# A decode attention kernel: SyncE's wait for the output moved behind the block, and W_O loaded in five pieces

## The chip, the cores and the metric

The kernel runs on one core of one Trainium2 chip, as one launch. The metric is the device time of that launch in microseconds (us); of several runs the median is taken. A profiled execution is one more run, with a trace; its span reaches from the first to the last instruction of the program.

The core has five engines that work beside each other: TensorE (PE in the profile, its weight loads PEld), VectorE (DVE), ScalarE (ACT), GpSimd (POOL) and SyncE (SP). [...] Transfers between the chip's memory and the on-chip buffers are issued by SyncE or ScalarE, run on 16 DMA engines, and add 16 to a semaphore when all of their data have landed.

## The reference

One token for each of four sequences (B = 4, D = 512) passes a layer norm and then an attention branch and a gated feed-forward branch in parallel; the output is the sum of the input and of both branches. Attention has 32 query heads on 8 key/value heads of 128, over the last 4096 positions of a cache of 16384.

```python
x  = A_x
xn = layernorm(x)
q  = (xn @ wq)  -> [4, 32 heads, 1, 128]
k, v = the last W = 4096 positions of k_cache, v_cache, each kv head used by 4 query heads
p  = softmax(q @ k^T * 128**-0.5)
attention   = (p @ v) -> [4, 1, 4096] @ wo        # wo: 4096 x 512
feedforward = (silu(xn @ w_gate) * (xn @ w_up)) @ w_down   # F = 1792
out = x + attention + feedforward                 # [4, 1, 512], bf16
```

## The kernel before

The keys and values of two sequences and one kv head make one step; there are ND = 16 steps. A step's keys are 2 MB and its values 2 MB, each loaded with one transfer into one half of a double buffer (`kbuf`, `vbuf`). TensorE turns the keys (`transposes`), VectorE copies them out of PSUM, TensorE forms the scores against the queries, VectorE finds the row maximum, ScalarE takes the exponential, and TensorE multiplies with the values (`pv`). TensorE and VectorE run this in a loop of eight rounds of two steps, one step behind each other in a software pipeline.

All weights and all keys and values are issued by SyncE, in the order in which its function in the block is written: W_Q, two steps of keys, the two feed-forward weights W_gate and W_up, then values and keys in turn, each behind the wait that frees its half buffer, then W_down, the last step's values in two halves, and W_O. No scheduler moves anything: every engine's order is the order of its function.

W_O is held as 32 rows of 512 elements in each of 128 partitions (4 MB; a row is 1 KB in a partition and 128 KB in all). `WO_CUTS` (L120) says where it is cut. Before, the cuts (0, 16, 26, 30, 32) make four pieces of 16, 10, 4 and 2 rows. Each piece is one transfer (`load_wo`, L227 to L229) with a semaphore of its own, `d_wo[n]`. At the end of TensorE's function (L479 to L486) a loop over the 32 rows waits for a piece where a cut stands, and adds two matmuls for each row (the two halves of the 512 output columns) into `ps_acc`, which already holds the input and the feed-forward branch. Behind the first piece four unneeded matmuls (`spin`) fill a pause.

When the last matmul is done (`s_acc`), VectorE casts `ps_acc` into `y` (L349), and SyncE (L247) and ScalarE (L267) issue one output transfer each, of 2 KB. Both add 16 to `d_out`, and SyncE waits for 32 (L248) as the last step of its function. The wait on L248 is carried by the branch with which SyncE leaves the block; the profile shows it with line 171.

Behind the five functions the block (`with nc.Block()`, L171) ends with a barrier: each of the other engines drains and adds to a semaphore, GpSimd collects these, and then releases all. In the profile all of this has line 171. The program's first barrier, ahead of the block, has line 500.

Of the kernel before, what the change touches and what calls it, by code (L numbers as in the profile page):

```python
# [10 lines left out]
def bass_parallel_sum__sliding_block_cached__swiglu_ffn__decode_kernel(  # L11
# [10 lines left out]
    out: bass.AP,  # L22
):
    B, _, D = A_x.shape
    _, HKV, Sk, Dh = A_k_cache.shape
    HQ = A_wq.shape[1] // Dh
    F = B_w_gate.shape[1]
# [84 lines left out]
    def sem(name):  # L112
        return nc.alloc_semaphore(name=name)
# [3 lines left out]
    d_wu = sem("d_wu")  # L117
    d_wd = sem("d_wd")
    d_out = sem("d_out")
    WO_CUTS = (0, 16, 26, 30, 32)  # L120
    d_wo = [sem("d_wo%d" % q) for q in range(len(WO_CUTS) - 1)]
    d_k = [sem("d_k%d" % s) for s in range(2)]
    d_v = [sem("d_v%d" % s) for s in range(2)]
# [43 lines left out]
    def kv_ap(cache, d):  # L167
        b0 = d % 2 * 2
        return cache[b0:b0 + 2, d // 2, Sk - W:, :].rearrange("b (q t) d -> q b (t d)", t=NT)

    with nc.Block() as block:  # L171
# [40 lines left out]
        @block.sync  # L212
        def _(eng):
            def load_k(d):
                if d >= 2:
                    eng.wait_ge(s_tr, 2 * NG * (d - 1))
                eng.dma_start(KB[:, d % 2 * KVN:(d % 2 + 1) * KVN], kv_ap(A_k_cache, d)).then_inc(d_k[d % 2], 16)

            def load_v(d):
                eng.wait_ge(s_pv, d + 1)  # L220
                eng.dma_start(VB[:, d % 2 * KVN:(d % 2 + 1) * KVN], kv_ap(A_v_cache, d)).then_inc(d_v[d % 2], 16)

            def load_v_half(d, h, done):
                a = d % 2 * KVN + h * HKN
                eng.dma_start(VB[:, a:a + HKN], kv_ap(A_v_cache, d)[:, :, h * HKN:(h + 1) * HKN]).then_inc(done, 16)  # L225

            def load_wo(n):  # L227
                a, b = WO_CUTS[n], WO_CUTS[n + 1]
                eng.dma_start(WO[:, a:b, :], wo_ap[:, a:b, :]).then_inc(d_wo[n], 16)  # L229

            eng.dma_start(WQ[:], wq_ap).then_inc(d_wq, 16)
            load_k(0)
            load_k(1)
            eng.dma_start(WG[:], wg_ap).then_inc(d_wg, 16)
            eng.dma_start(WU[:], wu_ap).then_inc(d_wu, 16)
            load_v(0)
            for d in range(2, ND):
                load_k(d)
                load_v(d - 1)
            eng.dma_start(WD[:], wd_ap).then_inc(d_wd, 16)  # L240
            eng.wait_ge(s_pv, ND)
            load_v_half(ND - 1, 0, d_v[1])
            load_v_half(ND - 1, 1, d_vz)
            for n in range(len(d_wo)):
                load_wo(n)
            eng.wait_ge(s_y, 1)
            eng.dma_start(out_ap[0], y[0:B, :]).then_inc(d_out, 16)  # L247
            eng.wait_ge(d_out, 32)  # L248

        @block.scalar  # L250
        def _(eng):
# [100 lines left out]
        def _(eng):  # L352
# [67 lines left out]
            def spin(n):  # L420

                for _ in range(n):
                    mm(ps_S[0][:], ident[:], KB[:, 0:512], start=True)
# [55 lines left out]
            for c in range(NO):  # L479
                if c == WO_CUTS[1]:  # L480
                    spin(4)
                if c in WO_CUTS:
                    eng.wait_ge(d_wo[WO_CUTS.index(c)], 16)
                for n in range(2):
                    last = mm(ps_acc[64 * n:64 * n + B, 0:256], OP[:, c, :], WO[:, c, 256 * n:256 * n + 256])
            last.then_inc(s_acc, 1)  # L486


# [1 line left out]
_INS = ['A_x', 'A_k_cache', 'A_v_cache', 'A_wq', 'A_wo', 'B_x', 'B_w_gate', 'B_w_up', 'B_w_down']  # L490
_OUTS = [((4, 1, 512), 'bfloat16')]
# [23 lines left out]
```

## Time and profile before

| what | value |
|---|---|
| time, median of 3 runs | 197.37 us (197.1 to 197.96) |
| the profiled execution's own time | 196.87 us |
| its span, first to last instruction | 195.1 us |
| mean granted TensorE clock | 0.991 |
| bytes read from memory | 81.01 MB, 415 GB/s over the span |
| busy share of the span: PE, PEld, DVE, ACT, POOL | 83%, 72%, 59%, 9%, 5% |

The page has the busy shares, the span in 40 slices, and the chain of work that ended last. Its time starts at the span's start. In the tables of instructions a line such as L354 is that of a helper (`mm`), so groups are told apart by what they write and read: `ps_acc<-wo_sb,oP` are the matmuls with W_O. "SPq" and "ACTq" are the sequencers of SyncE and ScalarE, where issues of transfers, drains, branches and semaphore instructions stand. A number in square brackets behind an instruction is the idle time of its engine before it, and what ended that.

### The profile page before, as it was taken

The numbers are of one execution on the slowest core, as the hardware profiler recorded it, in microseconds if no ns is written. First come the engines' busy times: TensorE is split into PE (matmuls) and PEld (weight loads), VectorE is DVE, ScalarE is ACT, GpSimd is POOL, SyncE is SP. The second block draws the span as 40 slices with busy tenths as digits, with TensorE's granted clock in tenths as the row PEclk, the third lists the DMA queues.
The fourth block names the chain that finished last, engine by engine and source line by source line (L and its number), as shares of the span: only waits on it lengthen the run. The fifth ranks groups of instructions, "written<-read, shape, count | busy, mean of one in ns | idle before, by whom it ended". The sixth has DMA issues, their size and how long they took to land.

```text
span 195.1 us, 7758 instructions
## 1 busy us (share of the span) xinstructions
PE 162.7 (83%) x3466; PEld 140.2 (72%) x3467; DVE 114.9 (59%) x250; ACT 16.6 (9%) x26; POOL 10.3 (5%) x23
## 2 busy tenths in 40 slices
PE   0127999379898989898989898989898989898995
PEld 0113898368887888788878787878787878786752
DVE  1005777237676767676767676767676767675610
ACT  5600101001010101010101010101010101010000
POOL 8930000000000000000000000000000000000000
PEclk9999999789999999999999999999999999999999
DMA  6999999999999999999999999999999999999991
GB/s 222 430 430 430 432 420 437 421 430 430 430 433 430 433 433 430 433 430 433 433 437 430 430 430 430 430 430 430 430 430 430 430 433 433 430 428 420 438 407 68
DMA packets 5934, 81.10 MB, mean 416 GB/s; under 512 B 668, under 2 KB 680, under 8 KB 936
## 3 DMA queue, kind: packets, MB, share of 16 engines
q1 hardware_dynamic: 5912, 81.01, 97.4%
q8 instruction: 5, 0.08, 0.1%
q10 hardware_dynamic: 16, 0.01, 0.0%
q14 instruction: 1, 0.01, 0.0%
HBM read 81.01 MB, written 0.00 MB: 415 GB/s over the span
## 4 chain that ended last, share of the span: by engine, by line
DMA 63%; PE 32%; issue 1%; DVE 1%; SPq 1%; DVEq 0%
DMA kbuf<-in_A_k_cache_dram 48%; PE ps_kt L382 16%; DMA wo_sb<-in_A_wo_dram 9%; PE ps_s L354 8%; DMA wq_sb<-in_A_wq_dram 6%; PE ps_o L354 5%; PE ps_acc L354 2%; PE ps_kt L354 2%; DVE kT L294 1%; SPq L225 1%; DVE kT L282 0%; SPq L229 0%; DVE y_sb L349 0%; DVE qz L285 0%; DVEq L293 0%
## 5 line engine op out<-in xcount | busy, mean ns | idle before, releaser
L294 DVE COPY kT<-ps_kt 128x1024 bf16<-128x1024 bf16 x128 | 79.5, 683 | 25.3 <-PE ps_kt L382 25.3
L382 PE MATMUL ps_kt<-ident,kbuf 128*128 128x128 bf16 x1024 | 62.8, 219 | 10.6 <-DMA kbuf<-in_A_k_cache_dram 10.6
L382 PEld LDWEIGHTS ps_kt<-ident,kbuf 128*128 128x128 bf16 x1024 | 57.3, 98 | 15.8 <-issue 15.7
L354 PE MATMUL ps_o<-p,vbuf 128*128 128x64 bf16 x1120 | 39.2, 195 | 0.0
L354 PEld LDWEIGHTS ps_o<-p,vbuf 128*128 128x128 bf16 x1120 | 36.0, 99 | 1.1
L354 PEld LDWEIGHTS ps_s<-qz,kT 128*128 128x128 bf16 x1024 | 31.7, 98 | 6.7 <-issue 3.6
L354 PE MATMUL ps_s<-qz,kT 128*128 x1024 | 34.9, 192 | 1.3
L299 DVE TENSOR_REDUCE rm<-ps_s 128x8 bf16<-128x512 f32 x17 | 11.8, 692 | 23.7 <-PE ps_s L354 23.7
L263 ACT ACTIVATE p<-ps_s 128x512 bf16<-128x512 f32 x17 | 10.1, 597 | 162.1 <-PE ps_s L354 162.1
L354 PE MATMUL ps_o<-p,ones 128*128 128x128 bf16 (+1 forms) x69 | 7.1, 225 | 4.6 <-DMA vbuf<-in_A_v_cache_dram 3.2
L354 PEld LDWEIGHTS ps_o<-p,ones 128*128 128x128 bf16 x69 | 4.6, 100 | 5.6 <-DMA vbuf<-in_A_v_cache_dram 3.4
L354 PE MATMUL ps_kt<-wq_sb,xnT 128*32 128x512 bf16 x32 | 3.4, 610 | 5.2 <-DMA wq_sb<-in_A_wq_dram 5.2
L359 PE MATMUL ps_acc<-i,xn 4*128 4x4 f32 x4 | 0.6, 254 | 7.4 <-ACT xn L260 7.4
L354 PE MATMUL ps_s<-mkc,mkr 2*128 2x512 bf16 x17 | 6.5, 385 | 0.0
L354 PE MATMUL ps_s<-dg,ones 8*128 8x512 bf16 x17 | 6.5, 385 | 0.0
L354 PEld LDWEIGHTS ps_kt<-wq_sb,xnT 128*32 128x32 bf16 x32 | 1.3, 140 | 6.8 <-issue 6.8
L282 DVE STREAM_TRANSPOSE kT<-ps_kt 128x512 f32<-128x512 f32 x2 | 1.4, 718 | 7.8 <-PE ps_kt L354 7.8
L359 PEld LDWEIGHTS ps_acc<-i,xn 4*128 4x128 f32 x4 | 0.6, 207 | 7.3 <-issue 7.3
L310 DVE TENSOR_REDUCE den<-ps_o 128x8 f32<-128x128 f32 x18 | 4.9, 274 | 1.0 <-PE ps_o L354 1.0
L207 POOL MEMSET vbuf<- 128x6144 f32 x1 | 5.2, 5222 | 0.0
L304 DVE TENSOR_REDUCE m<-ps_acc 8x1 f32<-8x128 f32 x17 | 4.6, 269 | 0.3 <-PE ps_acc L354 0.3
L314 DVE TENSOR_TENSOR oT<-ps_o,den 128x8 f32 (+1 forms) x18 | 3.0, 167 | 2.9 <-issue 2.7
(67 smaller groups left out, 50.0 us busy)
## 6 DMA issues: line engine op xcount, KB each, us to landing
kbuf<-in_A_k_cache_dram SPq DMA_DIRECT2D x16, 2048.0 KB, 12.6
vbuf<-in_A_v_cache_dram SPq DMA_DIRECT2D x15, 2048.0 KB, 11.3
wq_sb<-in_A_wq_dram SPq DMA_DIRECT2D x1, 4096.0 KB, 12.3
vbuf<-in_A_v_cache_dram SPq DMA_DIRECT2D x2, 1024.0 KB, 9.2
wo_sb<-in_A_wo_dram SPq DMA_DIRECT2D x1, 2048.0 KB, 14.4
wg_sb<-in_B_w_gate_dram SPq DMA_DIRECT2D x1, 1792.0 KB, 25.7
wu_sb<-in_B_w_up_dram SPq DMA_DIRECT2D x1, 1792.0 KB, 29.3
wd_sb<-in_B_w_down_dram SPq DMA_DIRECT2D x1, 1792.0 KB, 15.0
```

Of the source, the lines that this page charges most:

```text
L207: eng.memset(VB[:, HKN:].bitcast(FP32), 0.0)
L225: eng.dma_start(VB[:, a:a + HKN], kv_ap(A_v_cache, d)[:, :, h * HKN:(h + 1) * HKN]).then_inc(done, 16)
L263: eng.activation(P[:, d % 2 * PS:d % 2 * PS + SN], ps_S[d % 2][:], ACT.Exp, scale=SCALE).then_inc(s_p, 1)
L282: eng.transpose(qT[:, 512 * n:512 * n + 512], ps_kt[n][:])
L294: eng.tensor_copy(KT[:, u * HKN + 1024 * g:u * HKN + 1024 * (g + 1)], kt_ps[g].rearrange("p a b -> p (a b)")).then_inc(s_ev, 1)
L299: eng.tensor_reduce(RM[:], ps_S[bank][:].rearrange("p (t c) -> p c t", c=C), AX.X, ALU.max).then_inc(s_rm, 1)
L304: eng.tensor_reduce(m8[:], mt_ps, AX.X, ALU.max)
L310: eng.tensor_reduce(den[:], den_ps.rearrange("p (t c) -> p c t", c=C), AX.X, ALU.add)
L314: eng.tensor_tensor(OT[:, 2 * b:2 * b + 2, ds(r * REP, REP)], O_ps.rearrange("p (j h) -> p j h", j=2), den[:].rearrange("p (j h) -> p j h" ...
L354: return eng.matmul(o, l, r, start=start, stop=stop, skip_group_check=True)
L359: last = eng.transpose(xT_ps[:, c * B:(c + 1) * B], xn[:].rearrange("b (p c) -> b c p", c=NC)[:, c, :], I4[:])
L382: last = eng.transpose(kt_ps[g][:, k, :], KB[:, a:a + 128], ident[:])
```

## The change

Two edits. `WO_CUTS` gets five pieces, of 16, 10, 3, 2 and 1 rows, so there is one more transfer, one more semaphore and one more wait in TensorE's loop. And SyncE's wait for `d_out` leaves SyncE's function in the block and stands behind the block, so SyncE passes the block's closing barrier first and waits for the output afterwards.

```diff
@@ -117,7 +117,7 @@
     d_wu = sem("d_wu")
     d_wd = sem("d_wd")
     d_out = sem("d_out")
-    WO_CUTS = (0, 16, 26, 30, 32)
+    WO_CUTS = (0, 16, 26, 29, 31, 32)
     d_wo = [sem("d_wo%d" % q) for q in range(len(WO_CUTS) - 1)]
     d_k = [sem("d_k%d" % s) for s in range(2)]
     d_v = [sem("d_v%d" % s) for s in range(2)]
@@ -245,7 +245,6 @@
                 load_wo(n)
             eng.wait_ge(s_y, 1)
             eng.dma_start(out_ap[0], y[0:B, :]).then_inc(d_out, 16)
-            eng.wait_ge(d_out, 32)
 
         @block.scalar
         def _(eng):
@@ -486,6 +485,9 @@
             last.then_inc(s_acc, 1)
 
 
+    nc.sync.wait_ge(d_out, 32)
+
+
 # ---- launch: one core; inputs and outputs as the reference has them ----
```

## The prediction

> **What bounds the kernel now.** I read the page of the profile first: its span, the row of DMA shares and the chain of work that ended last.
>
> ```profile
> span 195.1 us, 7758 instructions
> DMA  6999999999999999999999999999999999999991
> GB/s 222 430 430 430 432 420 437 421 430 430 430 433 430 433 433 430 433 430 433 433 437 430 430 430 430 430 430 430 430 430 430 430 433 433 430 428 420 438 407 68
> DMA 63%; PE 32%; issue 1%; DVE 1%; SPq 1%; DVEq 0%
> ```
>
> The DMA engines are at 90% or more in 38 of the 40 slices, and the chain is made of transfers for 63%. The kernel streams its data; nothing in the diff changes how many bytes are moved. So only two places can move the time: the last transfers, and what follows them. The chain of work cut to the last stretch shows both ends of that.
>
> ```profile
> 173.79 16.83 DMA wo_sb<-in_A_wo_dram
> 190.62 0.04 issue
> 190.66 2.23 PE ps_acc L354 x32
> 192.89 0.02 issue
> 192.92 0.43 DVE y_sb L349
> ```
>
> The timeline of the same stretch (start, duration, engine, line, operation, count) gives the pieces of W_O one by one. The idle time in brackets stands before the first matmul of a piece and is ended by the landing of that piece.
>
> ```profile
> 187.65 1.91 PE L354 MATMUL ps_acc<-wo_sb,oP 128*4 128x256 bf16 x32
> 190.66 0.96 PEld L354 LDWEIGHTS ps_acc<-wo_sb,oP 128*4 128x4 bf16 x20 [0.62 <-DMA wo_sb<-in_A_wo_dram]
> 190.66 2.21 PE L354 MATMUL ps_acc<-wo_sb,oP 128*4 128x256 bf16 x32
> 191.89 0.31 PEld L354 LDWEIGHTS ps_acc<-wo_sb,oP 128*4 128x4 bf16 x8 [0.27 <-DMA wo_sb<-in_A_wo_dram]
> 192.49 0.09 PEld L354 LDWEIGHTS ps_acc<-wo_sb,oP 128*4 128x4 bf16 x4 [0.29 <-DMA wo_sb<-in_A_wo_dram]
> 192.92 0.43 DVE L349 CAST y_sb<-ps_acc 128x256 bf16<-128x256 f32 x1 [5.54 <-PE ps_acc L354]
> 193.37 0.35 SPq L247 DMA_DIRECT2D out_dram<-y_sb  x1
> 193.38 0.28 ACTq L267 DMA_DIRECT2D out_dram<-y_sb  x1
> ```
>
> TensorE waits for each of the pieces of 10, 4 and 2 rows. The end is therefore: last piece lands (192.49), four matmuls, the cast to y, two output transfers issued at 193.37, their landing, and the barrier that closes the block. That barrier is line 171; its instructions (ns as min/median/max, then first and last start) are the last ones of the trace:
>
> ```profile
> L171 POOLq EVENT_SEMAPHORE  x2: 17/17/17, 195.0 to 195.0; - x2
> L171 ACTq DRAIN  x1: 241/241/241, 193.7 to 193.7; - x1
> L171 SPq COMPARE_BRANCH  x1: 33/33/33, 194.8 to 194.8; - x1
> L171 SPq DRAIN  x1: 13/13/13, 194.9 to 194.9; - x1
> L171 SPq EVENT_SEMAPHORE  x1: 17/17/17, 195.1 to 195.1; - x1
> L171 PEldq EVENT_SEMAPHORE  x1: 51/51/51, 195.1 to 195.1; - x1
> ```
>
> SyncE's branch out of the block carries the wait for d_out and starts at 194.8, when the output has landed. Only then come its drain (194.9), GpSimd's collecting and releasing (195.0) and the five engines' leave (195.1). SyncE's own waits, from the table of waits, say the same in sums:
>
> ```profile
> SPq L247 <- DVE y_sb L349: 18.2, 1, 18.2
> SPq L171 <- DMA out_dram<-y_sb: 1.0, 1, 1.0
> SPq L500 <- PEq L500: 0.7, 1, 0.7
> SPq L171 <- PEq L171: 0.2, 1, 0.2
> ```
>
> **Part one: the wait behind the block.** In the instruction order of the changed program SyncE's branch has no wait, and the wait for d_out is the last instruction in its list, behind the barrier. Nothing is queued behind it on SyncE inside the program, and no other engine waits for it there. What moves: SyncE issues the output at 193.37 for 0.35 us, branches at about 193.72 and reaches its drain at about 193.76. ScalarE's drain, which comes straight behind an issue of the same kind, started at 193.7, took 241 ns and so ended at 193.94, 0.8 us before the output had landed: a drain does not wait for a transfer. I give SyncE's drain the same 241 ns in place of the 13 ns it took when the transfer was over: 194.0. From SyncE's drain to the release the barrier takes 0.2 us, so everyone leaves at 194.2. The output lands at 194.8 as before (0.6 us of cover; were the landing 0.6 us quicker, the barrier would be late instead and the saving would shrink to nothing). SyncE then passes one wait instruction, priced like its other one at 17 ns. The span ended at 195.1, the last instruction being TensorE's of 51 ns; 194.8 to that end is 0.35 us, less 0.02 for the wait instruction: **0.33 us saved in the span**.
>
> There is a second part, outside every view. The profiled execution's own time is 196.87 us with a span of 195.1, so 1.77 us lie before the first and behind the last instruction. Now all five engines come to what follows the program at the same moment, 195.1. After the change four come at 194.2 and SyncE alone at about 194.8. Whatever those four do by themselves before they meet SyncE again then lies beside its wait. No view shows this. Its lower bound is 0 (SyncE has the longest way by itself, or they do not meet). The nearest row for the upper bound is the program's first barrier, line 500: SyncE, the first there, waited 0.7 us for the others to get through it. I take the middle, **0.35 us**, since no row is nearer to one end, and keep 0 and 0.7 for the range. [...]
>
> **Part two: the pieces of 3, 2 and 1 rows.** The sizes and the time to landing of the pieces as they are:
>
> ```profile
> wo_sb<-in_A_wo_dram SPq DMA_DIRECT2D x1, 512.0 KB, 17.6
> wo_sb<-in_A_wo_dram SPq DMA_DIRECT2D x1, 256.0 KB, 17.7
> L229 SPq DMA_DIRECT2D wo_sb<-in_A_wo_dram x4: 432/432/601, 173.1 to 174.7; - x4
> L354 PE MATMUL ps_acc<-wo_sb,oP x64: 269/272/273, 187.7 to 192.6; 128*4 128x256 bf16 x64
> 189.00:190.00 1.00, 1.00 (x15) 0.50 (x10) 0.00 (x0) 0.00 (x0) 0.00 (x0) 1.00 0.97 399
> ```
>
> One more issue on SyncE costs 0.43 us at about 175.1. It is hidden: SyncE then waits 18.2 us for y, and the pieces land 17 us after their issue, so their transfers are far behind the issue. No queue of ScalarE or GpSimd changes.
>
> On TensorE the last piece now brings two matmuls in place of four. A row of W_O is a pair of matmuls; 16 rows took 1.91 us of which the last pair is 0.27, so a row adds (1.91 - 0.27) / 15 = 0.11 us. **0.11 us saved** if the last piece lands when it did. The row before it must then be done: the piece of two rows lands about 0.3 us (one row of transfer, below) earlier and needs 0.22 us of steps, so it is out of the way, with 0.08 to spare. The added wait, for d_wo[4], sits in front of those last two matmuls and holds nothing else back.
>
> Against that stands what a fifth piece costs the transfers. From the starts above, the piece of 4 rows came 1.23 us after the one before it, that of 2 rows 0.60 us after that. By size alone a row is (1.23 - 0.60) / 2 = 0.315 us, which leaves 0.60 - 0.63 = -0.03 us as the fixed cost of a piece: none. The change also makes runs shorter (3 KB, 2 KB and 1 KB in place of 4 KB and 2 KB), and no run of 1 KB of a weight is in this trace. The window from 189 to 190 us (last row: length, busy time of PE, PEld, DVE, ACT and POOL, clock, DMA share, GB/s), in which the shorter runs begin, still moved 399 GB/s at 97% busy, that is 411 at full share; the page gives 430 for most slices, so shorter runs lose at most some 5 to 7%. On the last 6 rows (1.9 us) that is 0 to 0.13 us; I take the middle, **0.06 us lost**. Net for the pieces: 0.05 us saved, between 0.14 saved and 0.02 lost.
>
> **The sum.** 0.33 + 0.35 + 0.05 = 0.73 us off 196.87: 196.14 us for that execution. It lies 0.50 us below the median of the runs (197.37), so I set the sum against the median: 197.37 - 0.73 = **196.64 us**, or 0.37% less. A measurement of this kernel can tell about 0.5%, 0.99 us, from no change: the forecast is "within 0.5%".
>
> **Rivals.** *Only the span gains.* What follows the program is not shortened, because SyncE's own way to the meeting point is the longest. For it: SyncE is the only engine that comes late. Against it: at line 500 SyncE was the early one. 0.33 + 0.05 = 0.38 us: 196.99 us. Also here belongs a change that does not do what it says: a SyncE drain that waits for its own transfer, against which ScalarE's 241 ns stand; that would leave 0.05 us, 197.32.
>
> *The whole of the other engines' spread is hidden.* The four take 0.7 us behind the program as at line 500, and SyncE little: 0.33 + 0.70 + 0.05 = 1.08 us, 196.29 us. For it: every instruction with which SyncE leaves a barrier is short (17 ns, TensorE's 51). Against it: the 0.7 us contain GpSimd's constants, which the end does not have. With 0.14 for the pieces it would be 1.17 us.
>
> *A fixed cost for each piece, on the path.* This one ends slower. If the last pieces were paid one after another, each with the latency of a transfer, the last landing would come later by what the output transfer shows from issue to landing, 194.8 - 193.37 = 1.43 us, less the 0.11 of matmuls; with the gain in the span alone the sum is 1.43 - 0.11 - 0.33 = 0.99 us slower, 198.36 us. It decides from 0.44 us of extra landing time with the span's gain, and from 0.79 with the tail's too. The pieces of 4 and 2 rows speak against it: they came 1.23 and 0.60 us apart, in proportion to size. [...]
>
> **How the numbers follow.** Forecast 0.44; only the span, or less, 0.12; the whole spread hidden 0.36; fixed cost 0.08. The first two are within 0.5%, 0.56 together; the third is faster by more than that, 0.36; the fourth stands at the 0.99 us of the bound and goes to slower, 0.08. The range reaches over the first three cases with the runs' own spread of a few tenths (197.1 to 197.96 around 197.37): 196.0 to 197.4 us; the fixed cost and part of the tails stay outside.
>
> **What would show it.** Right: SyncE's drain of line 171 near 193.7 to 194.0, the releases of the other engines near 194.2, and SyncE's wait for the output as the last instruction, with a span near 194.7 and the time outside the span down from 1.77 to about 1.4 us; five issues of W_O; the last LDWEIGHTS group x2 with the wait before it ending within 0.1 us of 192.49. Wrong: a last piece at 192.9 or later (fixed cost), a SyncE drain that ends with the landing (no saving from the wait), a time outside the span that stays at 1.77 (only the span) or falls below 1.2 (more than I took).

## The result, and the profile after

The changed kernel took 196.33 us (median of 8 runs, 195.88 to 196.62), the kernel before beside it 197.45 us (median of 8 runs, 197.01 to 198.07). The ratio is 0.9947, with a 95% interval of 0.9932 to 0.9962: 1.05 us faster, between 0.75 and 1.34 (the two medians lie 1.12 us apart). That is 0.53%, just over the 0.5% that the prediction had named as the bound; its 196.64 us lies 0.31 us above the measured median.

The profiled execution of the changed kernel took 196.38 us, with this span and these shares in the chain of work that ended last:

```profile
span 195.1 us, 7759 instructions
DMA  6999999999999999999999999999999999999992
DMA 61%; PE 34%; issue 1%; DVE 1%; SPq 1%; DVEq 0%
```

The span is the same 195.1 us as before, though the time is shorter. Two things cancel in it, and the timeline of the end shows the first (start, duration, engine, line, operation, count, idle time before it):

```profile
188.18 1.91 PE L353 MATMUL ps_acc<-wo_sb,oP 128*4 128x256 bf16 x32 [0.54 <-DMA wo_sb<-in_A_wo_dram]
191.14 1.29 PEld L353 LDWEIGHTS ps_acc<-wo_sb,oP 128*4 128x4 bf16 x26 [0.57 <-DMA wo_sb<-in_A_wo_dram]
192.65 0.09 PEld L353 LDWEIGHTS ps_acc<-wo_sb,oP 128*4 128x4 bf16 x4 [0.22 <-DMA wo_sb<-in_A_wo_dram]
192.97 0.08 PEld L353 LDWEIGHTS ps_acc<-wo_sb,oP 128*4 128x4 bf16 x2 [0.23 <-DMA wo_sb<-in_A_wo_dram]
193.28 0.42 DVE L348 CAST y_sb<-ps_acc 128x256 bf16<-128x256 f32 x1 [5.92 <-PE ps_acc L353]
193.74 0.35 SPq L247 DMA_DIRECT2D out_dram<-y_sb  x1
193.74 0.28 ACTq L266 DMA_DIRECT2D out_dram<-y_sb  x1
```

In this execution already the first piece of W_O, which the change leaves alone, came late: TensorE waited 0.54 us for it and started at 188.18, against 187.65 before. The second piece came at 191.14 against 190.66, and the output was issued at 193.74 against 193.37. Behind the issue the order is new. The instructions of the block's closing barrier, and the one behind it (ns as min/median/max, first and last start):

```profile
L171 POOLq EVENT_SEMAPHORE  x2: 17/17/17, 194.3 to 194.4; - x2
L171 ACTq DRAIN  x1: 241/241/241, 194.1 to 194.1; - x1
L171 SPq DRAIN  x1: 168/168/168, 194.1 to 194.1; - x1
L171 SPq EVENT_SEMAPHORE  x1: 17/17/17, 194.5 to 194.5; - x1
L171 PEldq EVENT_SEMAPHORE  x1: 51/51/51, 194.5 to 194.5; - x1
```

```profile
L488 SPq EVENT_SEMAPHORE  x1: 17/17/17, 195.1 to 195.1; - x1
```

SyncE drains at 194.1, all engines leave the barrier at 194.5, and the last instruction of the span is SyncE's wait at 195.1. From the issue of the output to the end of the span it was 195.1 - 193.37 = 1.73 us before and is 195.1 - 193.74 = 1.36 us now: 0.37 us less. SyncE's waits show the cover that was left:

```profile
SPq L247 <- DVE y_sb L348: 18.1, 1, 18.1
SPq L488 <- DMA out_dram<-y_sb: 0.6, 1, 0.6
SPq L171 <- PEq L171: 0.2, 1, 0.2
```

When SyncE had passed the barrier it still waited 0.6 us for the output, where it had waited 1.0 us ahead of the barrier. And the time outside the span, 196.87 - 195.1 = 1.77 us before, is 196.38 - 195.1 = 1.28 us.

### The profile page after: what moved, and what is told of

Same layout as the page of the kernel before. It is cut to its first block, busy times and chain, and to the rows that moved or that the text cites. A ratio compares the mean times of both kernels' runs of the same rounds, so it can differ in the third digit from the quotient of the medians.

```text
span 195.1 us, 7759 instructions
## 1 busy us (share of the span) xinstructions
PE 164.4 (84%) x3466; PEld 141.5 (73%) x3467; DVE 115.4 (59%) x250; ACT 16.6 (9%) x26; POOL 10.3 (5%) x23
## 4 chain that ended last, share of the span: by engine, by line
DMA 61%; PE 34%; issue 1%; DVE 1%; SPq 1%; DVEq 0%
DMA kbuf<-in_A_k_cache_dram 46%; PE ps_kt L381 17%; DMA wo_sb<-in_A_wo_dram 9%; PE ps_s L353 8%; DMA wq_sb<-in_A_wq_dram 6%; PE ps_o L353 5%; PE ps_kt L353 2%; PE ps_acc L353 2%; DVE kT L293 1%; SPq L225 1%; DVE kT L281 0%; SPq L229 0%; DVE y_sb L348 0%; DVE qz L284 0%; DVEq L292 0%
## 5 line engine op out<-in xcount | busy, mean ns | idle before, releaser
L381 PE MATMUL ps_kt<-ident,kbuf 128*128 128x128 bf16 x1024 | 65.4, 224 | 10.5 <-DMA kbuf<-in_A_k_cache_dram 10.4
L381 PEld LDWEIGHTS ps_kt<-ident,kbuf 128*128 128x128 bf16 x1024 | 59.9, 100 | 15.8 <-issue 15.7
L353 PE MATMUL ps_o<-p,vbuf 128*128 128x64 bf16 x1120 | 38.4, 193 | 0.0
L353 PEld LDWEIGHTS ps_o<-p,vbuf 128*128 128x128 bf16 x1120 | 35.2, 98 | 1.1
```

The lines of the kernel that those rows point to most:

```text
L353: return eng.matmul(o, l, r, start=start, stop=stop, skip_group_check=True)
L381: last = eng.transpose(kt_ps[g][:, k, :], KB[:, a:a + 128], ident[:])
```

## The experiments

The first theory was the prediction's, with its open term read from the trace after: the wait saves 0.37 us in the span and 0.5 us outside it, the pieces almost nothing. The rivals: the pieces carry most of the gain, or any waiting engine would do as well as SyncE, or each piece has a fixed cost. The ratios are to the kernel before on the same chip, with 95% intervals; "outside" is the mean over the runs of time less span, which is 1.73 and 1.74 us for the kernel before in the two sets.

| run | ratio to before | median us | before us | outside us |
|---|---|---|---|---|
| wait only | 0.9965 (0.9947 to 0.9982) | 196.27 | 197.11 | 1.24 |
| wait only, again | 0.9968 (0.9950 to 0.9986) | 196.42 | 197.20 | 1.25 |
| pieces only | 0.9982 (0.9967 to 0.9997) | 196.94 | 197.11 | 1.75 |
| the change again | 0.9956 (0.9932 to 0.9981) | 196.30 | 197.20 | 1.27 |
| TensorE waits | 0.9973 (0.9957 to 0.9989) | 196.60 | 197.11 | 1.56 |
| rows 16 to 31 singly | 0.9979 (0.9967 to 0.9991) | 196.81 | 197.11 | 1.27 |
| pieces 16, 10, 5, 1 | 0.9972 (0.9955 to 0.9989) | 196.70 | 197.20 | 1.27 |

**The wait alone.** The changed kernel with the old cuts.

```diff
-    WO_CUTS = (0, 16, 26, 29, 31, 32)
+    WO_CUTS = (0, 16, 26, 30, 32)
```

> The wait behind the block, W_O in the old four pieces. Theory 1 (the wait saves about 0.37 us in the span and about 0.5 us outside it, the pieces next to nothing): ratio 0.9957, between 0.994 and 0.997, time outside the span 1.3 us. Rival (the wait saves only the barrier in the span, and the five pieces the rest of the 1.12 us): ratio 0.998, outside the span 1.7 us or more.

The ratio is 0.9965, the medians lie 0.84 us apart, and the time outside the span falls to 1.24 us as in the full change. From the issue of the output to the end of the span its profile has 194.9 - 193.52 = 1.38 us, again some 0.35 us less than before. The rival, in which the tail stays at 1.7 us, is out. The same kernel was run again in the second set:

> The wait behind the block with the old four pieces, once more. Theory 1: 0.85 us faster than before, ratio 0.9957 (0.9945 to 0.997), 1.27 us outside the span. Rival (the pieces carry 0.35 us, so the wait 0.7): ratio 0.9965.

It came out at 0.9968 and 0.78 us between the medians, with 1.25 us outside the span. The ratio lies nearer to the rival's, the difference of the medians nearer to the theory's; the interval holds both, so ratios alone do not part 0.7 from 0.85 us.

**The pieces alone.** The kernel before with the new cuts.

```diff
-    WO_CUTS = (0, 16, 26, 30, 32)
+    WO_CUTS = (0, 16, 26, 29, 31, 32)
```

> W_O in five pieces, SyncE's wait inside the block as before. Theory 1: ratio 0.9985 to 1.000 (0 to 0.3 us faster), time outside the span 1.77 us. Rival (the pieces carry most of it): ratio 0.996, 0.7 us faster. Second rival (a fixed cost for a fifth piece): slower, ratio 1.002 or more, the last piece's wait ending well behind the fourth's by more than 0.4 us.

The ratio is 0.9982, which is 0.35 us, the medians lie only 0.17 us apart, and the time outside the span is unchanged. There is a small gain, and no fixed cost of the size that the second rival needs. The timeline of this run gives the gain more sharply than the ratio does:

```profile
190.79 1.29 PEld L354 LDWEIGHTS ps_acc<-wo_sb,oP 128*4 128x4 bf16 x26 [0.73 <-DMA wo_sb<-in_A_wo_dram]
192.37 0.09 PEld L354 LDWEIGHTS ps_acc<-wo_sb,oP 128*4 128x4 bf16 x4 [0.29 <-DMA wo_sb<-in_A_wo_dram]
192.65 0.08 PEld L354 LDWEIGHTS ps_acc<-wo_sb,oP 128*4 128x4 bf16 x2 [0.19 <-DMA wo_sb<-in_A_wo_dram]
192.97 0.42 DVE L349 CAST y_sb<-ps_acc 128x256 bf16<-128x256 f32 x1 [5.57 <-PE ps_acc L354]
```

From the start on the second piece to the start on the last it is 192.65 - 190.79 = 1.86 us, where four pieces took 192.49 - 190.66 = 1.83: the fifth piece costs the transfers 0.03 us. (The other profiles agree: 1.81 to 1.84 us in the three with these four pieces, 1.83 to 1.86 in the four with five.) From the start on the last piece to the cast it is 0.32 us, against 0.43 with two rows: 0.11 us saved. The product of the two single changes, 0.9965 x 0.9982 = 0.9947, is the ratio of the full change, which fits two parts that add; with intervals of 0.3 us and more to each side it is no sharp test of that.

**The change again**, beside the wait alone, to size the pieces by runs.

> The changed kernel once more, beside the wait-only kernel on one chip, to size what the pieces add. Theory 1 (the wait 0.85 us, the pieces 0.1 us by the shorter last step on TensorE): 0.95 us faster than before, ratio 0.9950 (0.994 to 0.996), its median 0.1 us below that of the wait alone. Rival (the pieces carry 0.35 us, as the mean of the pieces-only runs had it): 1.2 us faster, ratio 0.9940, 0.35 us below the wait alone.

The ratio is 0.9956, and the median lies 0.12 us below that of the wait alone on the same chip (196.30 against 196.42). That is what theory 1 said, but the intervals of the two ratios overlap widely; the 0.1 us rests on the timelines, not on these ratios.

**Another engine waits.** TensorE, not SyncE, waits for the output behind the block.

```diff
-    nc.sync.wait_ge(d_out, 32)
+    nc.tensor.wait_ge(d_out, 32)
```

> The changed kernel, but TensorE instead of SyncE waits for the output behind the block. Theory 1 with its mechanism (what follows the program is a chain through the engines in which TensorE is first and SyncE late, so only SyncE's lateness hides the others' steps): the span as in the changed kernel, the time outside it back up by 0.3 to 0.5 us to about 1.6 to 1.8, ratio to before 0.9965 to 0.998. Rival (any one engine that waits alone leaves the other four early, whichever it is): ratio 0.9947, outside the span 1.28 us.

The ratio is 0.9973 and the time outside the span 1.56 us. This instruction ends the span, and no engine but TensorE is late:

```profile
L488 PEldq EVENT_SEMAPHORE  x1: 51/51/51, 195.1 to 195.1; - x1
```

So it matters which engine waits: 0.3 of the 0.5 us outside the span are lost again. (The other three engines were not tried.) The trace's records of semaphore updates, which the views of the profile do not print, show where they go. Behind the program one semaphore that the kernel does not use is updated nine times in a row; these are the times of those updates in us from the start of each span (a time without its whole part has that of the time before it), with the end of the span and, for the two changed kernels, the start of the instruction that waited for the output:

```
before:          195.384 .419 .625 .669 .693 .799 .837 .871 .918
                 end of the span 195.145
changed:         194.851 .885 .996 195.040 195.255 .299 .337 .371 .419
                 SyncE's wait 195.120, end of the span 195.137
TensorE waits:   195.298 .332 .370 .414 .438 .544 .582 .616 .663
                 TensorE's wait 195.051, end of the span 195.102
```

In the changed kernel four updates come while SyncE still waits for the output, and the fifth 0.14 us after its wait. With TensorE as the one that waits, all nine come after its wait, from 0.25 us after it. That fits a chain in which the first update needs TensorE and the fifth needs SyncE. The chain is the author's estimate from these times and the difference between the two kernels; which engine makes which update is not recorded.

The size, however, is shown. The last of the nine comes 0.77 us behind the end of the span in the kernel before, 0.28 us in the changed kernel and 0.56 us with TensorE waiting: 0.49 and 0.21 us earlier. In the same three executions the time outside the span, taken to the ends given above, is 1.73, 1.24 and 1.53 us: 0.48 and 0.20 us less. So the whole gain outside the span is that these nine updates end earlier. The same semaphore gets nine more updates later on, and the last of them follows the last of the first nine by 1.14 to 1.15 us in all three executions; nothing is gained there.

The same semaphore has nine updates as the span begins, in the kernel before from -0.370 to 0.000 us, 24 to 46 ns apart but for one step of 112 ns. With TensorE waiting the nine behind the program take 0.365 us, 24 to 47 ns apart but for one step of 106 ns. Behind the program the kernel before has one more long step, of 206 ns ahead of the third update; what is late there the trace does not say.

**Sixteen single rows.**

```diff
-    WO_CUTS = (0, 16, 26, 29, 31, 32)
+    WO_CUTS = (0, *range(16, 33))
```

> The changed kernel with rows 16 to 31 of W_O in sixteen pieces of one row each: eleven... in all twelve pieces more than in the changed kernel, each with runs of 1 KB. Theory 1 (pieces cost almost nothing but some 5% of rate): last landing 0 to 0.15 us later than in the changed kernel, ratio to before 0.994 to 0.9955, with 17 issues on SyncE hidden. Rival (a fixed cost for each piece on the path, 0.1 us or more): 1.2 us or more later, ratio 1.000 or above.

There are seventeen pieces here, twelve more than in the changed kernel. The median is 0.54 us above that of the wait alone on the same chip, where the changed kernel should lie 0.1 us below it: some 0.6 us are lost, more than theory 1 said (0 to 0.15) and far less than the rival's 1.2 us. The last rows, one piece each, show the price:

```profile
192.36 0.09 PEld L353 LDWEIGHTS ps_acc<-wo_sb,oP 128*4 128x4 bf16 x2 [0.33 <-DMA wo_sb<-in_A_wo_dram]
192.70 0.08 PEld L353 LDWEIGHTS ps_acc<-wo_sb,oP 128*4 128x4 bf16 x2 [0.25 <-DMA wo_sb<-in_A_wo_dram]
193.01 0.08 PEld L353 LDWEIGHTS ps_acc<-wo_sb,oP 128*4 128x4 bf16 x2 [0.23 <-DMA wo_sb<-in_A_wo_dram]
193.37 0.08 PEld L353 LDWEIGHTS ps_acc<-wo_sb,oP 128*4 128x4 bf16 x2 [0.27 <-DMA wo_sb<-in_A_wo_dram]
```

They come (193.37 - 192.36) / 3 = 0.34 us apart, where a row in larger pieces took 0.315 us by the prediction's rows: 0.02 to 0.03 us for each piece. Twelve of them make some 0.3 us of the 0.6. The trace's records of landings, which the views do not print either, put most of the loss in the same place: from the last update of the first piece's semaphore to the last update of the last piece's it is 5.43 us here and 4.86 to 5.07 us in the other eight profiles. That is 0.36 to 0.57 us more, 0.03 to 0.05 us for each of the twelve. The slow issues described at the end are no likely cause: in each stretch of 2 us from 184 to 192 us the DMA engines had a busy share of 0.95 or more, so they had work.

**One row last, in four pieces.**

```diff
-    WO_CUTS = (0, 16, 26, 29, 31, 32)
+    WO_CUTS = (0, 16, 26, 31, 32)
```

> The changed kernel with four pieces of 16, 10, 5 and 1 rows. Theory 1 (TensorE needs 0.11 us for a row and a row's transfer 0.31 us, so five rows that land 0.31 us before the last one are not done when it lands): in the profile the cast starts 0.55 to 0.6 us after the last piece could land, there is no idle time before the last two matmuls, and the time is 0.1 to 0.25 us above that of the changed kernel. Rival (only the number of rows in the last piece matters): the same time as the changed kernel, with TensorE idle before the last two matmuls.

```profile
191.03 0.96 PEld L353 LDWEIGHTS ps_acc<-wo_sb,oP 128*4 128x4 bf16 x20 [0.56 <-DMA wo_sb<-in_A_wo_dram]
192.54 0.53 PEld L353 LDWEIGHTS ps_acc<-wo_sb,oP 128*4 128x4 bf16 x12 [0.54 <-DMA wo_sb<-in_A_wo_dram]
193.40 0.42 DVE L348 CAST y_sb<-ps_acc 128x256 bf16<-128x256 f32 x1 [5.85 <-PE ps_acc L353]
```

The last six rows run as one group of 12 loads with no idle time between the fifth and the sixth: the row that lands last finds TensorE busy. From the second piece's start to the cast it is 193.40 - 191.03 = 2.37 us, against 193.28 - 191.14 = 2.14 in the changed kernel, 0.23 us more, as expected. The last update of the last piece's semaphore came at 192.81, and the cast 0.59 us after it, within the 0.55 to 0.6 of theory 1. The median is 0.4 us above that of the change on the same chip, where 0.1 to 0.25 was expected; the intervals of the two ratios overlap, so the timeline is the better evidence. The short last piece pays only because the piece before it is short as well.

None of the other kernels has a better ratio to the kernel before than the changed kernel.

## Why the prediction was right or wrong

The direction and the mechanisms that carry the gain were right, and the time lies in the range. Term by term:

| term | predicted us | measured us |
|---|---|---|
| barrier beside the output's landing | 0.33 saved | 0.37 (1.73 to 1.36 from issue to end of span) |
| outside the span | 0.35 saved, 0 to 0.7 | 0.49 (1.77 to 1.28 profiled; 1.74 to 1.25 by runs) |
| two matmuls in place of four | 0.11 saved | 0.11 (pieces alone), 0.12 (profile after: 0.43 to 0.31) |
| transfers of a fifth piece | 0.06 lost, 0 to 0.13 | 0.00 to 0.03 lost (1.83 us to 1.83 and 1.86) |

The measured terms sum to 0.37 + 0.49 + 0.11 - 0.02 = 0.95 us, within the 0.75 to 1.34 us of the ratio's interval. The mis-sized term is the second one, the part behind the program that no view shows: the middle of 0 and 0.7 us stood for it and was 0.14 us short. It was that term, with the first one 0.04 us short and the fifth piece's cost some 0.04 us too high, that put the forecast at 0.37% and the larger chance on "within 0.5%". That 0.35 was a middle between two bounds and not worked out from a row, so that it came as near as it did is in part luck. The measured 0.53% (0.38 to 0.68%) stands across that bound, so the two cases with 0.56 and 0.36 were closer to each other than their chances said.

Of the steps: SyncE's drain took 168 ns straight behind its issue, priced at 241, and did not wait for its transfer; it ended 0.8 us before the output had landed. For the fifth piece the prediction's reason, a rate that falls with shorter runs, was not tested by itself; what the runs show is a small cost for each piece. The engines left the barrier 194.5 - 193.74 = 0.8 us after the issue of the output, as priced, and the cover of 0.6 us was the 0.6 us of SyncE's last wait. Of the rivals, the case of the span alone is out (1.24 to 1.27 us outside the span in every kernel whose SyncE waits behind the block). The case in which the whole spread of 0.7 us is hidden is out by its term, 0.49; by the time alone, 196.33 us, its 196.29 would have looked better than the forecast's 196.64. The fixed cost does not exist at the size that a slower result needed, by the prediction 0.44 us of extra landing time: for transfers queued behind others the price of smaller ones was low here, 0.02 to 0.05 us for a piece of 128 KB beside the 0.315 us of its data.

What the prediction did not foresee is that the pair of profiles would show the same span. W_O's first piece, which no edit touches, was late by half a microsecond in that execution. With it came the very sign that the prediction had named for a fixed cost, a last piece at 192.9 or later: it came at 192.97. But the time from the second piece to the last is the 1.83 us of before, so the lateness is that of the whole stream and not of the pieces. In other profiles TensorE waited for that piece too (0.28 us in the change run again, 0.26 us in the kernel with 16, 10, 5 and 1 rows) or not at all (wait alone, pieces alone). Runs of one kernel spread by as much, 195.88 to 196.62 us for the change. Why the stream of transfers ends earlier in some executions was not tried and stays open.

## What to carry to other kernels

In a kernel that ends like this one, the last wait for the output's landing belongs behind the closing barrier, not ahead of it (alone it gave 0.84 and 0.78 us between the medians): then the barrier, and part of what follows the program, lie beside the landing (0.37 and 0.49 us here). It should stand on the engine whose lateness hides most, here SyncE of the two that were tried (1.25 us outside the span, 1.56 with TensorE), and by the prediction's sum its part in the span is saved only as long as the landing outlasts the barrier, here by 0.6 us; no run here had a shorter landing. Cut the end of the last weight so that each piece is used up before the next one lands (five rows ahead of the last one cost 0.23 us here), and stop when the last piece is one step of the consumer; what is saved is the steps left after the last landing, here a tenth of a microsecond.

## What the runs showed of the hardware that was not expected

The time outside the span differed with the engine that came late: 1.74 us with all engines together, 1.56 with TensorE late, 1.25 with SyncE late. With SyncE late, four of the nine updates behind the program came ahead of its wait; with TensorE late, none. That a late engine hides the steps of those ahead of it in a chain is the author's estimate from these numbers.

The landing of a piece of W_O was not one moment. By the trace's records its semaphore got sixteen updates, and those of the last piece of W_O in the kernel before came from 190.72 us on, half of them by 191.16, the last at 192.45; TensorE started on the piece at 192.49. In all nine profiles the first and the last of the sixteen lie 1.6 to 2.0 us apart (for the last piece 1.73 before, 1.83 after). That is more than the two edits save together, and no run here tried to make it smaller.

Issues on SyncE were not all short. Of the seventeen W_O pieces in the kernel with single rows the issues took this long (ns as min/median/max, first and last start):

```profile
L229 SPq DMA_DIRECT2D wo_sb<-in_A_wo_dram x17: 432/433/3654, 173.4 to 187.9; - x17
```

Three were long, 1.57, 2.72 and 3.65 us by the trace's records one by one, and the last began at 187.9, where five issues were over by 175.7 in the changed kernel (last start 175.2, at most 0.6 us each):

```profile
L229 SPq DMA_DIRECT2D wo_sb<-in_A_wo_dram x5: 432/432/602, 173.1 to 175.2; - x5
```

The expectation had called them hidden. SyncE's wait for y shrank from 18.1 us to 5.8 us, so they were still over in time. What held them back was not tried.
